# Loading q in two transfers over 128 partitions in place of four over 32

## The chip, the cores and the metric

The kernel runs on one core of a Trainium2 chip. The metric is the device time of one execution in microseconds; less is better. The engines are named as in the profile: PE (matrix multiply; PEld is its weight load), DVE, ACT and POOL (elementwise work), and SP, which computes nothing here and issues the DMA transfers. An engine's name with a q behind it (SPq) means its instruction queue. Transfers are carried by 16 DMA engines that all queues share.

## The reference

Causal attention with a decay for each head and no softmax, for 8 batches of 8 heads, 576 positions and 64 columns; then a feed-forward layer with a squared relu over the 4608 tokens (8 x 576) of 512 columns:

```
scores = scale * np.matmul(q, k.transpose(0, 1, 3, 2))
gamma = 1.0 - 2.0 ** (-5.0 - np.arange(H, dtype=np.float32))
rel = pos[:, None] - pos[None, :]
Dmat = np.where(rel >= 0, gamma[:, None, None] ** rel[None, :, :], 0.0)
ret = scores * Dmat[None, :, :, :]
return np.matmul(ret, v).astype(np.float32)
...
h = x @ w_in
r = np.maximum(h, 0.0)
g = r * r
return (g @ w_out).astype(np.float32)
```

Inputs and output are fp32. w_in is 512 x 2048, w_out 2048 x 512.

## The kernel before

**Units and groups.** The tokens are cut into 36 units of 128 tokens with all 8 heads. A batch has four full units and a tail of 64 positions; the tails of two batches share a unit. So there are 32 full units and 4 tail units. Two units make a group, 18 groups in all. Attention goes chunk by chunk: within a unit the masked scores, and a state R that carries the sum of k times v from chunk to chunk.

**How a unit comes in.** The first 8 units are loaded in pairs (lines 430 to 449) and transposed on PE. The other 28, 24 full and 4 tails, go through `add_load` (lines 411 to 428): SP issues transfers of k, q and v into a slice of the tile `loads`, which has room for five units. Then POOL makes fp16 of it: k by L497 and q by L512 (a multiplication with the decay, two calls of L508 for a tail) into the tile `kq`, v by L518 into `v`. Then SP issues a DMA transpose of `kq` into `kqT` (L529). PE reads `kqT` for the scores (`psc`) and for what comes from the state (`psO`), and `kq` and `v` for the sums of the state (`psS`), all through the helper at L483.

**The layout of q.** For k and v a partition is a token (L422), 8 rows of 256 B for each partition. For q of a full unit the partition 32j + r holds, for the heads j and j + 4, the four tokens 4r to 4r + 3. In HBM four tokens of one head lie together, so each partition is filled by two rows of 1 KB, one of each head. In the slice of `loads` the first half of a partition belongs to the heads 0 to 3 (a = 0), the second to the heads 4 to 7 (a = 1). The layout stays through the transpose and is undone when the result is copied (L889).

**Order.** The order of all work is written out in the list `ORDER`: each entry is a task, each engine executes its tasks in that order, and a task of SP is the whole load of one tensor of one unit. So SP's queue is one fixed sequence of loads, transposes (L529) and stores of the output (L1001, L1006), in which an instruction that waits holds up all behind it. The task of a transpose waits for the POOL tasks of k and q of its unit. The weights come by POOL's queue. SP's transfers take eight semaphores in turn, and each transfer first waits for the one before it on its semaphore, so for the transfer eight places ahead in SP's queue.

**Feed-forward.** The layer is computed group by group, with a recursive seven-product scheme for the second matrix (L1304) and for some of the first (L1058; else L1209), ACT and DVE squaring and adding in between. Its matmuls are placed among the attention of later groups, so PE has work of a group at hand while it is to begin the scores of another, but always in the order of the list.

Of the kernel before, what the change touches and what calls it, by code (L numbers as in the profile page):

```python
# [183 lines left out]
def kernel(  # L184
# [9 lines left out]
    nc = tc.nc  # L194
# [3 lines left out]
    P = 128  # L198
    NP = H // 2
# [199 lines left out]
    def dma_task(key, dur, fn, more=(), **kw):  # L399
        t = add("SP", key, dur, fn, deps=list(last_load) + list(more), **kw)  # L400
        last_load[:] = [t]
        return t
# [8 lines left out]
    def add_load(u):  # L411
        kind, b, c = units[u]
        for n, (name, src) in enumerate((("k", k), ("q", q), ("v", v))):
            def fn(name=name, src=src):
                at = ((u - PAIRED) % LD * 3 + "kqv".index(name)) * H * D
                x = tile_of[name + "32", u] = loads[:, at:at + H * D].rearrange("p (h d) -> p h d", h=H)
                if kind == "full" and name == "q":
                    for j in range(NP):
                        nc.sync.dma_start(out=x[32 * j:32 * j + 32].rearrange("r (a t) d -> r a (t d)", a=2),  # L419
                                          in_=src[b, :, c * P:(c + 1) * P, :].rearrange("(a x) (r t) d -> x r a (t d)", a=2, t=4)[j])  # L420
                elif kind == "full":
                    nc.sync.dma_start(out=x, in_=src[b, :, c * P:(c + 1) * P, :].rearrange("h p d -> p h d"))  # L422
                else:
                    for i in range(2):
                        nc.sync.dma_start(out=x[i * 64:(i + 1) * 64],
                                          in_=src[b + i, :, 512:576, :].rearrange("h p d -> p h d"))
            behind_pair = T["kvx", 6] if PAIRED + 3 <= u < PAIRED + LD else []
            loaded[name, u] = dma_task(0, QL if name == "q" and kind == "full" else 2.2 if (u, name) == (PAIRED, "k") else 1.2, fn, acq=("ld" + name,), more=behind_pair)
# [1023 lines left out]
```

## Time and profile before

| | us |
|---|---|
| three runs | 282.50, 283.57, 286.36 |
| their median | 283.57 |
| the profiled execution, its time | 283.93 |
| its span, first to last instruction | 282.0 |

From the page and its lists, about the steps that the change touches:

| what | value |
|---|---|
| L419, q of 24 full units | 96 transfers of 64 KB; issue 339/427/3097 ns (least, median, most); to landing 1.9/3.4/6.0 us |
| L422, k and v of 24 full units | 24 transfers of 256 KB each; median to landing 4.9 and 4.2 us |
| L425, q of 4 tail units | 8 transfers of 128 KB; median to landing 3.4 us |
| L529, transposes | 28; issue 1232/1517/3114 ns; to landing 3.1/4.4/6.5 us |
| L512 on POOL | 24, median 1045 ns |
| packets on all queues | 119154, 50.03 MB |

How to read it: busy shares are means over the span. A line of the timeline gives start, length, engine, line, operation, and out<-in by the program's names. The chain of waits is followed back from the last instruction; its share of an engine is time in which that engine's work stood between the start and the end. The ends of matmuls are modelled, so PE's busy time may hide short waits. The granted clock of TensorE is 1.00 in every stretch looked at. The DMA share is the recorded time of packets over 16 engines; the records can overlap, so that it may go over 1.

### The profile page before, as it was taken

The page shows a single profiled execution, that of the slowest core. Times are in us where ns is not written, and L with a number is a line of the kernel's source. Part 1 is how long each engine was busy: PE and PEld are TensorE (multiplying, and loading weights), DVE is VectorE, ACT ScalarE, POOL GpSimd, SP SyncE. Part 2 cuts the span into 40 slices and gives each one's busy share as a digit, 9 for nine tenths or more (in the row PEclk, how much of TensorE's full clock was granted, in tenths as well). Part 3 has the DMA queues.
Part 4 walks back from the last instruction along what each step waited for, and adds up shares of the span by engine and source line. Part 5 has one row for each costly group of instructions (what it writes and reads, how often), then busy time and mean ns, then how long its engine had stood idle before and what let it go on. Part 6 is the DMA issues. An engine that isn't in the chain of part 4 may idle for free.

```text
span 282.0 us, 11585 instructions
## 1 busy us (share of the span) xinstructions
PE 273.1 (97%) x4726; PEld 237.5 (84%) x4726; DVE 198.0 (70%) x405; ACT 198.4 (70%) x374; POOL 100.9 (36%) x133
## 2 busy tenths in 40 slices
PE   8989999999999999989999999999999999999994
PEld 3567767888899888979998889898989999999983
DVE  4783379988988568586757595777597777565662
ACT  5657977577578965857797775686888485887831
POOL 7560036353655251455264343365265310000000
PEclk9999999999999999999999999999999999999999
DMA  6999998799999799999979999889979840022114
GB/s 192 300 201 208 246 323 192 171 231 164 195 166 212 166 178 209 222 178 165 230 169 212 195 200 207 210 183 245 182 197 219 155 114 2 5 84 105 40 74 149
DMA packets 119154, 50.03 MB, mean 177 GB/s; under 512 B 94784, under 2 KB 113728, under 8 KB 119104
## 3 DMA queue, kind: packets, MB, share of 16 engines
q1 hardware_dynamic: 114560, 44.84, 74.3%
q0 software_dynamic: 4224, 4.19, 9.1%
q8 instruction: 39, 0.64, 1.0%
q10 hardware_dynamic: 320, 0.26, 0.4%
q14 instruction: 11, 0.09, 0.1%
HBM read 36.70 MB, written 9.44 MB: 164 GB/s over the span
## 4 chain that ended last, share of the span: by engine, by line
PE 63%; DMA 16%; SPq 10%; DVE 4%; POOL 2%; issue 2%; ACT 1%; POOLq 0%; DVEq 0%; ACTq 0%
PE po L1304 28%; PE ph L1209 15%; PE ph L1058 13%; DMA w_out<-in_moe_w_out_dram 5%; SPq L419 5%; DMA loads<-in_q_dram 4%; PE psO L483 3%; DMA pair_c<-in_v_dram 3%; SPq L441 2%; DMA stage<-in_q_dram 2%; DMA kqT<-kq 2%; DMA out_dram<-o 2%; SPq L422 1%; SPq L529 1%; PE psS L483 1%
## 5 line engine op out<-in xcount | busy, mean ns | idle before, releaser
L1209 PE MATMUL ph<-xT,w_in 128*128 128x256 f16 x640 | 83.0, 273 | 0.9 <-DVE xT L713 0.5
L1209 PEld LDWEIGHTS <-w_in 128*128 128x128 f16 x640 | 61.6, 98 | 9.5 <-DMA w_in<-in_moe_w_in_dram 0.5
L1219 ACT ACTIVATE gT<-ph 128x512 f16<-128x512 f32 x80 | 46.2, 597 | 15.6 <-PE ph L1209 15.5
L1304 PEld LDWEIGHTS <-gT 128*128 128x128 f16 x544 | 51.1, 98 | 6.0 <-issue 0.3
L1304 PE MATMUL po<-w_out,gT 128*128 128x256 f16 x272 | 44.8, 273 | 0.0
L1304 PE MATMUL po<-wT,stage 128*128 128x256 f16 x272 | 42.5, 273 | 0.0
L1304 PEld LDWEIGHTS <-stage 128*128 128x128 f16 x408 | 38.1, 98 | 4.6 <-issue 0.2
L1304 PE MATMUL po<-wT,gT 128*128 128x256 f16 x272 | 40.8, 273 | 0.2 <-DVE o L1330 0.2
L1226 ACT ACTIVATE gT<-gT 128x512 f16<-128x512 f16 x66 | 40.0, 631 | 0.4
L497 POOL CAST kq<-loads 128x512 f16<-128x512 f32 x28 | 19.2, 687 | 54.0 <-DMA loads<-in_k_dram 49.6
L1101 ACT ACTIVATE gT<-gT 128x1024 f16<-128x1024 f16 x32 | 33.6, 1059 | 2.7 <-DVE gT L1087 2.6
L512 POOL TENSOR_TENSOR kq<-loads,qexp 128x512 f16<-128x512 f32 x24 | 26.8, 1116 | 22.1 <-DMA loads<-in_q_dram 21.8
L1058 PEld LDWEIGHTS <-pair_c 128*128 128x128 f16 x512 | 32.6, 98 | 1.3 <-issue 0.2
L518 POOL TENSOR_TENSOR v<-loads,vdec_full 128x512 f16<-128x512 f32 x24 | 27.4, 1146 | 10.7 <-DMA loads<-in_v_dram 10.6
L1277 DVE TENSOR_TENSOR stage<-gT,stage 128x512 f16<-128x512 f16 (+1 forms) x51 | 27.9, 561 | 0.8
L1087 DVE CUSTOM_DVE_ANT_0 gT<-ph,parts 128x512 f16<-128x512 f32 x24 | 16.5, 688 | 15.5 <-PE ph L1058 8.1
L1058 PEld LDWEIGHTS <-w_in 128*128 128x128 f16 x384 | 24.7, 98 | 1.2 <-issue 0.4
L1087 DVE CUSTOM_DVE_ANT_0 gT<-ph,stage 128x512 f16<-128x512 f32 x24 | 16.4, 686 | 12.8 <-PE ph L1058 12.3
L1330 DVE TENSOR_TENSOR o<-po,u 128x256 f32<-128x256 f32 x33 | 13.9, 421 | 15.2 <-ACT u L1320 4.7
L889 ACT CAST xT<-psO 128x512 f16<-128x512 f32 x28 | 15.9, 588 | 11.3 <-PE psO L483 11.2
L1320 ACT COPY u<-po 128x256 f32<-128x256 f32 x34 | 12.7, 374 | 12.2 <-PE po L1304 11.4
L1304 PE MATMUL po<-w_out,stage 128*128 128x256 f16 x136 | 21.2, 273 | 0.0
(111 smaller groups left out, 421.8 us busy)
## 6 DMA issues: line engine op xcount, KB each, us to landing
out_dram<-o SPq DMA_DIRECT2D x32, 256.0 KB, 3.1
loads<-in_k_dram SPq DMA_DIRECT2D x24, 256.0 KB, 4.9
loads<-in_q_dram SPq DMA_DIRECT2D x96, 64.0 KB, 3.4
loads<-in_v_dram SPq DMA_DIRECT2D x24, 256.0 KB, 4.2
w_in<-in_moe_w_in_dram POOLq DMA_DIRECT2D x4, 512.0 KB, 8.1
w_out<-in_moe_w_out_dram POOLq DMA_DIRECT2D x4, 512.0 KB, 14.4
pair_c<-in_k_dram SPq DMA_DIRECT2D x2, 512.0 KB, 5.5
pair_c<-in_q_dram SPq DMA_DIRECT2D x4, 256.0 KB, 6.1
```

Of the source, the lines that this page charges most:

```text
L497: op(out=out_.rearrange("p (n b a d) -> p n b a d", n=2, b=2, a=2), in_=in_.rearrange("p (a n b) d -> p n b a d", n=2, a=2))
L512: nc.gpsimd.tensor_tensor(out=out_.rearrange("p (t a d) -> p a t d", t=4, a=2), in0=tile_of["q32", u].rearrange("p (a t) d -> p a t d", a= ...
L518: nc.gpsimd.tensor_tensor(out=t, in0=tile_of["v32", u], in1=vdec[kind].rearrange("p (h o) -> p h o", o=1).to_broadcast([P, H, D]), op=ALU. ...
L889: (nc.scalar.copy if X_ENG[c] == "ACT" else nc.vector.tensor_copy)(out=tile_of["x", g].rearrange("p n (s e r t) -> p e (n s) r t", s=n, e= ...
L1058: nc.tensor.matmul(out_[:, e], lhsT=left[:, m, fi * P:(fi + 1) * P], rhs=right()[:, m], start=fresh and e == 0 and m == 0, stop=m == HK - ...
L1087: nc.vector._custom_dve(TENSOR_ADD_SAT, out=g_at(s, h, j), in0=bank(j, x), in1=part_at[name].rearrange("p (e t) -> p e t", t=P), s0=3.4028 ...
L1101: nc.scalar.activation(out=t, in_=t, func=ACTF.Square)
L1209: nc.tensor.matmul(tile_of["ph", g, fb][:, j, :], lhsT=w_in16[:, m, fi * P:(fi + 1) * P], rhs=tile_of["x", g][:, m, :], start=(m == 0), st ...
L1219: nc.scalar.activation(out=tile_of["g", g][:, nf * fb:nf * (fb + 1), :], in_=tile_of["ph", g, fb], func=ACTF.Relu)
L1226: nc.scalar.activation(out=t, in_=t, func=ACTF.Square)
L1277: (nc.gpsimd if eng == "POOL" else nc.vector).tensor_tensor(out=S_(k)(sl), in0=in0(sl), in1=in1(sl), op=op)
L1304: nc.tensor.matmul(tile_of["pb", g, bank], lhsT=left(i), rhs=right[:, i, :], start=(start and i == 0), stop=(i == HF - 1), skip_group_chec ...
```

## The change

For q of a full unit, the loop over the four head numbers j, each with 32 partitions and both halves, becomes a loop over the two halves a, each with all 128 partitions. The bytes, where they lie in HBM and where they go stay the same, as does everything else.

```diff
                 if kind == "full" and name == "q":
-                    for j in range(NP):
-                        nc.sync.dma_start(out=x[32 * j:32 * j + 32].rearrange("r (a t) d -> r a (t d)", a=2),
-                                          in_=src[b, :, c * P:(c + 1) * P, :].rearrange("(a x) (r t) d -> x r a (t d)", a=2, t=4)[j])
+                    for a in range(2):
+                        nc.sync.dma_start(out=x[:, NP * a:NP * a + NP].rearrange("p t d -> p (t d)"),
+                                          in_=src[b, :, c * P:(c + 1) * P, :].rearrange("(a x) (r t) d -> a x r (t d)", a=2, t=4)[a])
```

In the built programs, with counts from the slowest dimension to the fastest, one transfer of before goes from 32 x 2 x 256 elements in HBM to 32 x 2 x 256 in `loads`; one of the new goes from 4 x 32 x 256 to 128 x 1 x 256. SP issues 204 transfers in place of 252. On the other engines the instructions and their order are the same; what differs is the number of the semaphore that a transfer of SP raises, and that its readers wait for.

## The prediction

> **What bounds the kernel now.** First I read the page's totals, its slices of DMA and its chain.
>
> ```profile
> span 282.0 us, 11585 instructions
> PE 273.1 (97%) x4726; PEld 237.5 (84%) x4726; DVE 198.0 (70%) x405; ACT 198.4 (70%) x374; POOL 100.9 (36%) x133
> ...
> DMA  6999998799999799999979999889979840022114
> ...
> PE 63%; DMA 16%; SPq 10%; DVE 4%; POOL 2%; issue 2%; ACT 1%; POOLq 0%; DVEq 0%; ACTq 0%
> ```
>
> PE is all but full, yet the DMA row stands at 6 to 9 tenths up to slice 32 (to about 225 us), and the chain leaves PE for DMA and SPq over a quarter of the span. So two resources run side by side. The windows tell how close they are (columns: stretch, length, busy us and count of PE, PEld, DVE, ACT, POOL; granted clock; DMA share; GB/s).
>
> ```profile
> 80.00:100.00 20.00, 20.00 (x333) 18.27 (x330) 14.17 (x25) 17.43 (x32) 9.96 (x12) 1.00 1.05 179
> 100.00:120.00 20.00, 19.63 (x438) 18.02 (x436) 14.05 (x29) 13.95 (x25) 7.33 (x10) 1.00 1.13 206
> 120.00:140.00 20.00, 19.07 (x428) 17.24 (x426) 14.00 (x27) 14.16 (x30) 9.60 (x10) 1.00 1.03 193
> ```
>
> PE loses 2.2 us in all between 40 and 240 us (the ten windows of 20 us added up), most of it in the last two rows shown. The cause of that loss is in SP's timeline of one pair of units (start, length, line, form).
>
> ```profile
> 121.79 2.00 SPq L419 DMA_DIRECT2D loads<-in_q_dram  x4
> 123.84 0.43 SPq L422 DMA_DIRECT2D loads<-in_v_dram  x1
> 124.31 0.58 SPq L422 DMA_DIRECT2D loads<-in_k_dram  x1
> 124.93 3.18 SPq L419 DMA_DIRECT2D loads<-in_q_dram  x4
> 128.15 0.43 SPq L422 DMA_DIRECT2D loads<-in_v_dram  x1
> 128.68 0.52 SPq L1001 DMA_DIRECT2D out_dram<-o  x1
> 129.30 1.34 SPq L529 DMA_TRANSPOSE kqT<-kq  x1
> 130.69 0.57 SPq L422 DMA_DIRECT2D loads<-in_k_dram  x1
> 131.37 2.93 SPq L529 DMA_TRANSPOSE kqT<-kq  x1
> ```
>
> The second q load, issued from 124.93 us, landed at 130.07; POOL's L512 ran 130.23 to 131.27; the transpose was issued at 131.37 and landed at 136.76; the scores that read it began at 136.75. So q's load is just in time. The list of waits says the same (who waited for whom: us in total, times, longest).
>
> ```profile
> POOL kq L512 <- DMA loads<-in_q_dram: 21.8, 17, 4.5
> ...
> PE psc L483 <- DMA kqT<-kq: 1.3, 2, 0.9
> ```
>
> Elsewhere a unit's transpose lands earlier: the last one 4.8 us before its scores (227.5 against 232.4). That is the slack at the end.
>
> **What the change takes away.** 96 issues at L419 become 48. In the trace the 96 take 57.7 us of SP together (median 0.43 each, many held up by what is in flight). For the new ones the nearest rows are L441's, 128 partitions with one row each: 0.55 to 0.69 us where not held up. At 0.6, 48 cost 28.8, so SP is relieved of 28.9 us, 1.2 a unit. Every SP transfer also waits for the one eight places ahead of it (eight semaphores); with six transfers a unit instead of eight that wait reaches further back, and I cost it at nothing. None of this shortens PE's own work. At most the 2.2 us that PE loses from 40 to 240 us come back. Lower and upper bound of this part: -2.2 and 0.
>
> **What it adds.** Bytes and packets of data stay: 256 packets of 1 KB a unit, 6144 in all (packet records of the trace). What changes is how a transfer can be shared out. Each of the 252 transfers that SP issues has an outermost count of 32, 64 or 128 on both sides, and ends with sixteen 4-byte finishing packets (4480 on SP's queue: 252 times 16, and 16 more for each of 28 transposes), one to an engine. The new form has 128 partitions on one side, but 4 heads outermost on the other, of which each is 32 rows of 1 KB. No row of before has fewer than 16 outermost. From both sides: it is still split over 16 engines, as L441's is (32 outermost against 128), or over no more than the 4 equal parts that its outermost count gives. I take four, since all the rows shared out to 16 engines have a count that 16 divides, and this one hasn't.
>
> [...]
>
> Now the sum with four engines. Median durations in the packet records: 1 KB 46 ns, 256 B 18 ns, 2 KB 84 ns. A q load is 16 packets an engine now, 0.74 us; on four engines it is 64, 2.94 us, so 2.2 us more a unit, and 24 units put 53.0 us more on each of the four. Room for it: from 40 to 222 us (182 us) all packets at their median durations are 135.4 us an engine; as recorded, 180.0 us. The four then have 135.4 + 53.0 = 188.4 us to do, or, with q's packets at their recorded mean of 63 ns (24.2 us now, 96.8 then), 252.6. In the trace all 192 transfers of this stage whose landing it tells land in the order of their issue, so I take it that k, v, transposes and stores issued behind a q load wait for it on these four, and each is complete only with its last part. The stage of 182 us thus grows by 6.4 us at least and 70.6 at most.
>
> Which value: the recorded sum is too high, since records overlap (shares of 1.05 and 1.13 above, where an engine can't be more than full). The median sum is too low, since the engines also run dry while SP stands at a transpose for POOL: L529 waits 20.1 us for POOL (8.4 + 6.3 + 5.4 by line in the list of waits), with the next loads queued behind. Those waits stay, since each is for a q that lands no sooner. So 188.4 + 20.1 = 208.5, which is 26.5 more than 182. The slack of 4.8 at the end takes some off: 21.7. PE's order is fixed, and the 50 us after the last scores (232 to 282) are untouched, so this goes to the end whole. What hid q's load until now, PE's own 13.2 us a pair of units (scores at 61.1 and 232.4 us, 13 pairs apart), covers it no more: four engines need, at medians, 14.1 us a pair (1.15 each for k, v and transpose, 2.94 for q and 0.67 for the store, twice).
>
> Sum: 282.0 + 21.7 = 303.7 of span. SP's relief is already in the assumption that the engines are otherwise kept fed. The profiled execution took 283.93, 1.9 more than its span, so 305.6; its time is 0.4 above the median of 283.57. I say 306.
>
> **The rivals.**
> 1. Not slower: it is split over 16 engines all the same. For it: L441's sides differ too. Then a load of 128 KB lands as the tails' q loads do (128 KB, 3.4 us in the list of issues), and SP's relief brings 0 to 2.2 us: 281.4 to 283.6. It decides if the finishing packets stay 16 a transfer.
> 2. Four engines, but kept full throughout, the transposes' waits hidden by what is queued: 6.4 - 4.8 = 1.6 us, 285.
> 3. Four engines, at recorded durations: 70.6 - 4.8 = 65.8 more, 349. Against it: with the other twelve engines relieved of q, a packet meets less traffic.
> 4. Faster by more than 2%: SP is what holds PE. For it: SPq has 10% of the chain, L419 4.6% of it. Against it: 2.2 us of idle PE. If half of L419's 13 us of the chain came back, since the ends of matmuls are modelled and may hide waits, it were 277.
>
> **How the numbers follow.** The forecast has 0.80, rival 1 0.11, rival 2 0.04, rival 3 0.02, rival 4 0.03. Anything within 2%, some 5.7 us, of 283.6 can't well be told from no change: that is rivals 1 and 2, 0.15; faster 0.03; slower 0.82. Range: rivals 1, 2 and 4 are left below it (0.18 together), so it begins just above rival 2, at 286. Its upper end lies three quarters of the way from the least growth (6.4) to the most (70.6), since packets meet more traffic than their medians show and less than their means: 54.6 - 4.8 = 49.8 over 283.9, 334.
>
> **What would show it.** Page: 119154 packets become 117810 with four finishing packets a transfer, 118386 with sixteen. The q loads' 128 KB take over 5 us to landing rather than 3.4. PE's waits for kqT grow from 2.8 us (1.5 at the weight loads, 1.3 at the matmuls) to over 20, the scores' pairs are 14 to 16 us apart, and the DMA share falls although the kernel waits for DMA. I am wrong if the packets are 118386, or if PE waits for something other than kqT.

## The result, and the profile after

The changed kernel takes 306.07 us (median of four runs, 301.35 to 307.31) against 284.0 us before. Two of its runs, 307.31 and the profiled one of 306.83, are of a slower state, and every ratio here and below is of the fast runs alone: here 303.3 to 284.2 us, so 1.067, with a 95% interval of 1.050 to 1.085. The forecast was 306, slower by over 2%.

The page of the changed kernel, the parts that answer to those shown of before:

```profile
span 305.1 us, 11514 instructions
PE 281.9 (92%) x4726; PEld 242.7 (80%) x4726; DVE 203.0 (67%) x405; ACT 199.0 (65%) x374; POOL 100.4 (33%) x133
...
DMA packets 117811, 50.03 MB, mean 164 GB/s; under 512 B 93441, under 2 KB 112385, under 8 KB 117761
...
PE 49%; DMA 28%; SPq 12%; POOL 5%; ACT 2%; issue 2%; DVE 2%; POOLq 0%; ACTq 0%
```

The bytes are the same, and the packets are 117811. The prediction gave 117810 for four finishing packets a transfer and 118386 for sixteen, so 47 q transfers or more must have ended with four. The queues' count agrees: 3136 packets of 4 bytes on SP's queue in place of 4480, which is 48 x 4 instead of 96 x 16. The trace's records of packets, each with start and length, tell the same of the data: in the stage of the loads at least one 1 KB packet of a q load is under way for 90.4 us, and the most frequent number at a time is four (for 45.8 us). The chain lies on PE for 49% of the span instead of 63%, and on DMA for 28% instead of 16%.

The windows, with the columns of before:

```profile
80.00:100.00 20.00, 16.22 (x281) 14.59 (x279) 10.50 (x20) 11.54 (x19) 8.35 (x9) 0.83 1.06 156
100.00:120.00 20.00, 20.00 (x430) 18.28 (x428) 14.03 (x29) 14.24 (x30) 6.09 (x9) 1.00 1.00 185
120.00:140.00 20.00, 16.03 (x263) 13.97 (x261) 12.36 (x19) 12.04 (x22) 8.21 (x8) 0.91 0.98 151
```

PE now stands idle for about 4 us in two of these three stretches, and the granted clock falls in the same ones. The rate falls from 179 and 193 GB/s to 156 and 151, while the DMA share stays near 1: that share is a mean over 16 engines and doesn't tell that four have more to do than the rest.

SP's timeline, for the same pair of units as the one shown of before:

```profile
131.49 1.16 SPq L419 DMA_DIRECT2D loads<-in_q_dram  x2
132.70 0.48 SPq L422 DMA_DIRECT2D loads<-in_v_dram  x1
133.22 0.74 SPq L422 DMA_DIRECT2D loads<-in_k_dram  x1
134.01 3.94 SPq L419 DMA_DIRECT2D loads<-in_q_dram  x2
137.99 0.48 SPq L422 DMA_DIRECT2D loads<-in_v_dram  x1
138.57 1.08 SPq L1001 DMA_DIRECT2D out_dram<-o  x1
139.75 2.55 SPq L529 DMA_TRANSPOSE kqT<-kq  x1
```

The first two q transfers take 1.16 us to issue, as costed. The next two take 3.94, though half as many are issued as before; what holds SP there the profile doesn't name. So the relief of SP came to 9.8 us and not 28.9: L419 takes 47.9 us of SP over the run, before it took 57.7.

A stretch of the chain of waits (start, length, what) shows how that reaches PE:

```profile
149.52 3.65 SPq L419
...
153.21 5.52 DMA loads<-in_q_dram
...
158.86 0.51 POOL kq L512
...
159.86 1.04 POOL v L518
160.91 1.03 POOL kq L497
161.93 1.37 SPq L529
...
163.41 3.18 DMA kqT<-kq
...
166.64 0.32 PE psc L483 x16
```

It is 17 us from the issue of one q load to the scores, and 12.4 of them are that issue, its landing and the landing of the transpose. The cast of this q ended at 159.9 us, but its transpose was issued only at 163.41: from 159.58 SP stood in the issue of the transpose of the unit before, so the two other POOL casts in the chain aren't what it waited for.

### The profile page after: what moved, and what is told of

Read it like the earlier page. It is cut to its first block, busy times and chain, and to the rows that moved or that the text cites. A ratio compares the mean times of both kernels' runs of the same rounds, so it can differ in the third digit from the quotient of the medians.

```text
span 305.1 us, 11514 instructions
## 1 busy us (share of the span) xinstructions
PE 281.9 (92%) x4726; PEld 242.7 (80%) x4726; DVE 203.0 (67%) x405; ACT 199.0 (65%) x374; POOL 100.4 (33%) x133
## 2 busy tenths in 40 slices
DMA packets 117811, 50.03 MB, mean 164 GB/s; under 512 B 93441, under 2 KB 112385, under 8 KB 117761
## 4 chain that ended last, share of the span: by engine, by line
PE 49%; DMA 28%; SPq 12%; POOL 5%; ACT 2%; issue 2%; DVE 2%; POOLq 0%; ACTq 0%
PE po L1304 22%; PE ph L1058 11%; PE ph L1209 10%; DMA loads<-in_q_dram 9%; DMA kqT<-kq 5%; DMA loads<-in_k_dram 5%; SPq L419 5%; DMA w_out<-in_moe_w_out_dram 4%; SPq L422 3%; PE warm L392 2%; SPq L529 2%; DMA pair_c<-in_k_dram 2%; PE psO L483 2%; POOL kq L512 2%; DMA loads<-in_v_dram 1%
## 5 line engine op out<-in xcount | busy, mean ns | idle before, releaser
L1209 PEld LDWEIGHTS <-w_in 128*128 128x128 f16 x640 | 62.0, 98 | 9.3 <-issue 0.4
L1304 PEld LDWEIGHTS <-gT 128*128 128x128 f16 x544 | 51.9, 99 | 7.1 <-issue 0.6
L1304 PE MATMUL po<-w_out,gT 128*128 128x256 f16 x272 | 46.3, 280 | 0.0
L1304 PE MATMUL po<-wT,stage 128*128 128x256 f16 x272 | 44.2, 281 | 0.0
L1304 PEld LDWEIGHTS <-stage 128*128 128x128 f16 x408 | 38.8, 100 | 5.6 <-DVE stage L1277 0.3
L1277 DVE TENSOR_TENSOR stage<-gT,stage 128x512 f16<-128x512 f16 (+1 forms) x51 | 31.0, 620 | 0.8
L518 POOL TENSOR_TENSOR v<-loads,vdec_full 128x512 f16<-128x512 f32 x24 | 28.3, 1185 | 4.3 <-DMA loads<-in_v_dram 2.9
L1058 PEld LDWEIGHTS <-w_in 128*128 128x128 f16 x384 | 25.9, 101 | 1.3 <-issue 0.2
L483 PE MATMUL psc<-kqT 64*64 64x64 f16 (+1 forms) x576 | 10.7, 203 | 16.5 <-DMA kqT<-kq 15.3
L1087 DVE CUSTOM_DVE_ANT_0 gT<-ph,stage 128x512 f16<-128x512 f32 x24 | 16.4, 686 | 14.0 <-PE ph L1058 13.6
L483 PEld LDWEIGHTS <-kqT 64*64 64x64 f16 x576 | 7.8, 110 | 18.9 <-DMA kqT<-kq 16.4
```

Of the source, the lines that this page charges most:

```text
L483: t = nc.tensor.matmul(out_, lhsT=lhsT, rhs=rhs, start=start, stop=True, skip_group_check=True, tile_position=(64 * row, 64 * col))
L518: nc.gpsimd.tensor_tensor(out=t, in0=tile_of["v32", u], in1=vdec[kind].rearrange("p (h o) -> p h o", o=1).to_broadcast([P, H, D]), op=ALU. ...
L1058: nc.tensor.matmul(out_[:, e], lhsT=left[:, m, fi * P:(fi + 1) * P], rhs=right()[:, m], start=fresh and e == 0 and m == 0, stop=m == HK - ...
L1087: nc.vector._custom_dve(TENSOR_ADD_SAT, out=g_at(s, h, j), in0=bank(j, x), in1=part_at[name].rearrange("p (e t) -> p e t", t=P), s0=3.4028 ...
L1209: nc.tensor.matmul(tile_of["ph", g, fb][:, j, :], lhsT=w_in16[:, m, fi * P:(fi + 1) * P], rhs=tile_of["x", g][:, m, :], start=(m == 0), st ...
L1277: (nc.gpsimd if eng == "POOL" else nc.vector).tensor_tensor(out=S_(k)(sl), in0=in0(sl), in1=in1(sl), op=op)
```

## The experiments

**How many engines.** Three runs change the outermost count in HBM and nothing else about the bytes and packets of q. The first puts the 32 rows of a head outermost:

```diff
-                                          in_=src[b, :, c * P:(c + 1) * P, :].rearrange("(a x) (r t) d -> a x r (t d)", a=2, t=4)[a])
+                                          in_=src[b, :, c * P:(c + 1) * P, :].rearrange("(a x) (r t) d -> a r x (t d)", a=2, t=4)[a])
```

> Two transfers a q load, over all 128 partitions, as in the changed kernel, but with the 32 rows of a head outermost in HBM in place of the 4 heads (32 x 4 x 256 to 128 x 256). The tokens of q so land in other partitions than the readers take them from, so the output is that of another order of q; bytes, packets, instructions and their order are those of the changed kernel. Theory A (a transfer is shared out over as many engines as its outermost counts allow, and four engines are what costs the time): 16 engines again, 281 to 284 us, 118386 packets on the page, 16 finishing packets a transfer. Theory B (it is the form that costs: two transfers of 128 KB with unlike sides land later and are issued more slowly, however they are shared out): 300 to 306 us, as changed.

Measured 283.55 us, 0.999 of before (0.995 to 1.002). The DMA part of its page:

```profile
DMA packets 118386, 50.03 MB, mean 177 GB/s; under 512 B 94016, under 2 KB 112960, under 8 KB 118336
```

That is the count for sixteen finishing packets. It is two transfers of 128 KB over 128 partitions, in the same places of SP's queue as the changed kernel's, and the loss is gone. Theory B falls.

The second has eight outermost:

```diff
-                                          in_=src[b, :, c * P:(c + 1) * P, :].rearrange("(a x) (r t) d -> a x r (t d)", a=2, t=4)[a])
+                                          in_=src[b, :, c * P:(c + 1) * P, :].rearrange("h (a r t) d -> a h r (t d)", a=2, t=4)[a])
```

> Two transfers a q load over 128 partitions, each of 8 heads x 16 rows x 256 elements, so eight outermost. The tokens of q again land elsewhere, so the output is that of another order. Theory A: eight engines, 32 packets an engine and load, 1.47 us; the eight have 135.4 - 17.7 + 35.3 = 153.0 us to do, with SP's 20.1 of waits 173, under the 182 of the stage: 282 to 286 us, 118002 packets. Theory B: 300 to 306 us.

Measured 282.82 us, 0.996 of before (0.993 to 0.999), with the 118002 packets of eight:

```profile
DMA packets 118002, 50.03 MB, mean 178 GB/s; under 512 B 93632, under 2 KB 112576, under 8 KB 117952
```

So eight finishing packets a transfer, by my reading eight engines, carry it at no loss. The third goes back to four transfers of 64 KB, with two heads outermost in each:

```diff
                     for a in range(2):
-                        nc.sync.dma_start(out=x[:, NP * a:NP * a + NP].rearrange("p t d -> p (t d)"),
-                                          in_=src[b, :, c * P:(c + 1) * P, :].rearrange("(a x) (r t) d -> a x r (t d)", a=2, t=4)[a])
+                        for i in range(2):
+                            nc.sync.dma_start(out=x[64 * i:64 * i + 64, NP * a:NP * a + NP].rearrange("p t d -> p (t d)"),
+                                              in_=src[b, :, c * P:(c + 1) * P, :].rearrange("(a i x) (r t) d -> a i x r (t d)", a=2, i=2, t=4)[a, i])
```

> Four transfers a q load as before the change, of 64 KB each, but each over 64 partitions from 2 heads x 32 rows x 256 elements, so two outermost; q lands where it should. Theory A: two engines, 128 packets an engine and load, 5.9 us; the two have 135.4 - 17.7 + 141.3 = 259 us to do in place of 135.4, at least 72 us more than the 182 of the stage after the slack of 4.8, and 92 with SP's waits: 354 to 376 us, 117810 packets. Theory B: four transfers of 64 KB like before, 283 to 290 us.

Measured 358.25 us, 1.262 of before (1.255 to 1.268). Four transfers of 64 KB are as many and as large as before the change, so neither number nor size is the cause. The page has 117810 packets, which is two finishing packets for each of the 96 transfers, and while q's 1 KB packets are under way (147.3 us), two stand at a time for 111.9 us. PE's waits for the transposes, from its list of waits (its lines lie one further down):

```profile
PEld L484 <- DMA kqT<-kq: 45.6, 13, 8.5
PE psc L484 <- DMA kqT<-kq: 44.1, 13, 8.4
```

16, 8, 4 and 2 engines thus give 283.6, 282.8, 306.1 and 358.3 us: flat where the few engines' packets, at their medians, fit into the stage (153.0 of 182 us for eight), and steep where they don't (188.4 for four, 259 for two). Two engines have 259 us to do at the medians; from the first q issue at 39.9 us to the last transpose at 299.3 it took 259.4.

**A version that keeps two transfers and sixteen engines.** The rows are outermost as in the first run, and the readers follow: `qT` takes every fourth column, and the decay of q is built for that order.

```diff
+        if units[u][0] != "tail" and u >= PAIRED:
+            return t.rearrange("p n (r x) -> p n r x", x=NP)[:, :, 16 * c:16 * c + 16, x]
```

> Two transfers a q load over 128 partitions with the 32 rows outermost, and all readers adapted: the decay of q is built for that order at the start, and the scores and the state's part read q's columns with a step of four. Theory A: 280 to 284 us, at best 2.2 us under before, if the reads with a step cost PE nothing. Theory B: 300 to 306 us.

Measured 285.91 us, 1.007 of before (1.004 to 1.010): no gain. The scores on PE (the least, median and most ns of one, in that kernel's lines) tell why it isn't even equal:

```profile
L490 PE MATMUL psc<-kqT x576: 186/234/311, 10.1 to 236.1; 64*64 64x64 f16 x149, 64*64 64x128 f16 x43
```

Before the change the median of the same 576 was 193 ns. The reads with a step of four columns took longer here, PE's busy time is 278.3 us against 274.2 in the first run, and PE is what is full.

**Is it the engines' time, or only q's own landing?** k and v of the full units are read as 128 rows of 2 KB, on the changed kernel and on the one before:

```diff
-                    nc.sync.dma_start(out=x, in_=src[b, :, c * P:(c + 1) * P, :].rearrange("h p d -> p h d"))
+                    nc.sync.dma_start(out=x.rearrange("p h d -> p (h d)"), in_=src[b].rearrange("h (p e) d -> (h p) (e d)", e=8)[c * P:(c + 1) * P])
```

> The changed kernel, with k and v of the 24 full units read as 128 rows of 2 KB that lie together in HBM, in place of 1024 rows of 256 B: the same bytes, issues and order, but other tokens and heads reach the partitions, so the output isn't that of the reference's k and v. At the medians of the packet records that is 8 packets of 84 ns an engine and load, 0.67 us, in place of 1.15, so 23.0 us less on every engine over the 24 units. q's transfers stay as changed. Theory A1 (the four engines' time in all is the limit): 188.4 - 23.0 + 20.1 = 185.5 us of the 182, less than the slack: 283 to 288 us. Theory A2 (the engines have time to spare, and only q's own later landing counts, since SP and POOL wait for it in turn): 300 to 306 us, as changed.

> The kernel before the change with the same edit of k and v as in the run beside it, whose control it is; again other tokens and heads reach the partitions. Both theories: no limit of DMA is to be lifted beyond the 2.2 us that PE loses, so 281 to 284 us.

Measured 286.64 us (1.003 of before, 0.998 to 1.008) with the change, and 283.31 us (0.994, 0.990 to 0.998) without. q's transfers are those of the changed kernel, which by the packet count used four engines, with 64 packets on each for a load, and the loss falls from 6.7% to 0.3% (1.0% against its control) when k and v take 23 us less of these engines, at the packets' medians. So A1: it is the sum of what stands on the four. PE waits little for the transposes then:

```profile
PEld L483 <- DMA kqT<-kq: 3.4, 5, 1.4
...
PE psc L483 <- DMA kqT<-kq: 2.6, 3, 1.3
```

**What fills the time above the medians' sum.** The prediction put 20.1 us of SP's waits at the transposes on top of the 188.4. Six runs were meant to see whether that is so. In the first two, ACT's queue issues q, once with four engines and once with sixteen:

```diff
-                        nc.sync.dma_start(out=x[:, NP * a:NP * a + NP].rearrange("p t d -> p (t d)"),
+                        nc.scalar.dma_start(out=x[:, NP * a:NP * a + NP].rearrange("p t d -> p (t d)"),
```

> The changed kernel with the 48 q transfers issued by ACT's queue in place of SP's, so that they no longer stand behind a transpose that waits for POOL, nor k and v behind them in one queue; the work is the same. Theory C (the 20.1 us of the prediction's sum are engines run dry while SP stands at a transpose): much of them comes back, 286 to 296 us, if ACT can spare the issues (the control beside it tells). Theory D (the four engines are kept full, and what exceeds 188.4 us is packets that take longer than their median in the traffic): 300 to 306 us.

> The control for the run beside it: two transfers with the 32 rows outermost, so sixteen engines, issued by ACT's queue; the tokens of q land in other partitions, so the output is that of another order of q. Both theories: what ACT's 48 issues cost by themselves, 0.6 us each, 28.8 us of an engine that is busy 198 of 282: 282 to 290 us.

Measured 317.28 us (1.112, 1.103 to 1.120) and 291.76 us (1.031, 1.027 to 1.035). ACT's issues cost 8 us by themselves, more than expected, and neither theory had the first time. By the ratios the two are 8.1% of before apart, the changed kernel and the first run above 6.8%. But it isn't the same loss, as the waits of the first of the two show:

```profile
PE ph L1209 <- ACT xT L889: 6.9, 2, 5.1
...
PEld L483 <- DMA kqT<-kq: 2.0, 2, 1.3
...
PE psc L483 <- DMA kqT<-kq: 1.8, 2, 1.2
```

PE hardly waits for transposes there. It waits for ACT, 24 us in all, and ACT, which now issues q, itself waits 27.0 us for q's transfers (in the control not at all). So this pair decides nothing about theory C.

A cleaner one shortens what SP waits for: POOL's multiplications become casts.

```diff
-                nc.gpsimd.tensor_tensor(out=out_.rearrange("p (t a d) -> p a t d", t=4, a=2),
-                                        in0=tile_of["q32", u].rearrange("p (a t) d -> p a t d", a=2),
-                                        in1=by.rearrange("p (a t o) -> p a t o", a=2, o=1).to_broadcast([P, 2, 4, D]), op=ALU.mult)
+                nc.gpsimd.tensor_copy(out=out_.rearrange("p (t a d) -> p a t d", t=4, a=2),
+                                      in_=tile_of["q32", u].rearrange("p (a t) d -> p a t d", a=2))
...
-            nc.gpsimd.tensor_tensor(
-                out=t, in0=tile_of["v32", u],
-                in1=vdec[kind].rearrange("p (h o) -> p h o", o=1).to_broadcast([P, H, D]), op=ALU.mult)
+            nc.gpsimd.tensor_copy(out=t, in_=tile_of["v32", u])
```

> The changed kernel with POOL's two multiplications a full unit (L512 for q, L518 for v, 1.05 us each) replaced by plain casts of the same shapes (0.61 us by L497's row): the decay factors of q and v are left out. Each unit's transpose so waits up to 0.87 us less for POOL, 21 us over 24 units. Theory C (SP's waits for POOL at the transposes are what the four engines lose above 188.4 us): 288 to 298 us. Theory D (they are not): 302 to 306 us.

> The kernel before the change with the same plain casts on POOL, as the control for the run beside it; the decay factors of q and v of full units are left out here too. Both theories: 281 to 284 us, since PE's own work sets the end.

Measured 304.59 us (1.071, 1.065 to 1.077) and 284.51 us (1.001, 0.997 to 1.005). SP's waits at the transposes, as the lists of SP's own waits give them, first of the changed kernel, then of this one (the transpose is L526 here):

```profile
SPq L529 <- POOL v L518: 14.0, 8, 3.2
SPq L529 <- POOL kq L497: 10.4, 6, 3.9
SPq L529 <- POOL kq L512: 3.0, 3, 1.3
```

```profile
SPq L526 <- POOL kq L497: 8.1, 5, 3.4
SPq L526 <- POOL v L517: 6.8, 5, 2.8
SPq L526 <- POOL kq L512: 2.8, 4, 1.0
```

By these lists 27.4 us became 17.7, and the ratio stayed within its interval (1.071 against 1.067). But the lists give more than SP waited: the largest entry is v's cast, and a transpose waits for the casts of k and q alone. The same holds of the 8.4 + 6.3 + 5.4 us in the prediction, for instance at the transpose issued at 131.37 us before the change (start, length):

```profile
130.23 1.04 POOL L512 TENSOR_TENSOR kq<-loads,qexp 128x512 f16<-128x512 f32 x1
131.36 2.56 POOL L518 TENSOR_TENSOR v<-loads,vdec_full 128x512 f16<-128x512 f32 x2
```

The cast of its q was done at 131.27, and SP, free since 131.26, issued it 0.1 us later; the list puts 2.6 us down to v's casts, which ended during the issue. All 28 transposes of before start after their own casts, and in SP's timeline the gaps ahead of them that end with a cast are 2.5 us in all. They are 6.3 us with the change and 2.0 here. So theory C falls: there were no 20 us of such waits to lose.

Last, each transpose is issued as two:

```diff
-            nc.sync.dma_start_transpose(out=t, in_=tile_of["kq", u].rearrange("p x n -> p (x n)"))
+            for i in range(2):
+                nc.sync.dma_start_transpose(out=t[:, NP * i:NP * i + NP], in_=tile_of["kq", u][:, i])
```

> The changed kernel with each of the 28 transposes at L529 issued as two, one for k's half and one for q's, with the same packets; the result is the same. In the packet records of before, 435 packets of 256 B, some 16 a transpose, take over 200 ns each, 408 us together, so 25.5 us an engine; with the change 511 and 752 us. Theory H (each transpose holds every engine for about 0.9 us at its start, and that is what the four engines lose above 188.4 us): 28 starts more, so 20 to 25 us more, 322 to 332 us, and about 900 such packets. Theory D' (the hold is that of engines that wait for others, and costs the four nothing): 303 to 310 us.

> The kernel before the change with each transpose issued as two, as the control for the run beside it. Theory H: 135.4 us at the medians and twice 25.5 of holds are 186.4 on every engine, over the 182 of the stage but within the slack: 284 to 292 us. Theory D': 282 to 286 us.

Measured 316.82 us (1.113, 1.104 to 1.121) and 308.64 us (1.082, 1.074 to 1.089). Both lie outside what either theory gave. The long packets became fewer, not more: 326 over 200 ns with the change, 156 without. So they are no fixed hold at the start of a transpose, and theory H falls; theory D' fails in its times. The records do show what the long packets wait with: in the changed kernel those of one transpose begin up to 3.4 us apart and end within 60 ns of one another. One q load's packets stood from 54.9 to 58.6 us; seventeen long packets began between 55.7 and 56.9, four more at 58.3 to 58.5, and all ended at 59.0. That looks like the other engines waiting at a transpose for the four that still have q, though the records don't tell the engine.

What goes with the time of the second kernel is the issue of its transposes (SP, least, median and most ns):

```profile
L530 SPq DMA_TRANSPOSE kqT<-kq x56: 1188/1218/2202, 49.3 to 254.4; - x56
```

Half a transpose takes as long to issue as a whole one at its least (1232 ns before), so SP issues transposes for 72.7 us instead of 48.1, and the last of them is issued 30 us later (254.4 against 224.4). The 24.6 us more of issuing and the 24.2 us more of time agree, and no packet at all is under way for 11.7 us of the stage, 0.5 before. That SP's queue is what costs the time is argued from this; no run lengthened its issuing alone.

## Why the prediction was right

- *PE nearly full, q's load just in time.* Held, though not at once: the first two pairs of units on this path began their scores at 61.0 and 73.7 us (61.1 and 73.2 before), and PE's first wait for a transpose of the new loads ended at 90.7, after 3.7 us.
- *Four engines, by the outermost count of 4.* When it was taken no row had fewer than 16 outermost, so it was an estimate. The runs bear it out at the counts they had: with 32, 8, 4 and 2 outermost in HBM a q transfer ended with 16, 8, 4 and 2 finishing packets (118386, 118002, 117811 and 117810 packets on the pages); with 4 and 2, four and two packets of data were most often under way at a time (45.8 of 90.4 us, 111.9 of 147.3); and the times, 283.6, 282.8, 306.1 and 358.3 us, follow the work of the few. That a finishing packet stands for an engine is read from these together, as the records don't name the engine, and no run shows what other counts do.
- *SP's relief, 28.9 us of issuing, brings 0 to 2.2 us.* The gain held, the 28.9 didn't. With sixteen engines the relief is 15.9 us (L419 takes 41.8), and the time stays within its interval of before. With four it is 9.8.
- *The floor of 6.4 us and the ceiling of 70.6.* The stage grew by 25.2 us: the last transpose was issued at 249.6 us in place of 224.4. Predicted were 26.5. The eight-engine run agrees with the same sum: 153 of 182 us, and no loss. The two-engine run agrees with it to 0.4 us without any addition.
- *20.1 us for SP's waits at the transposes.* This step failed in its cause. Its size was right: the four had 188.4 us to do at the medians, and it took 209.3 from the first q issue (40.3) to the last transpose (249.6), 20.9 more. But the 20.1 us weren't waits: SP stood 2.5 us ahead of transposes for a cast of q, 6.3 with the change. With two engines the list has 20.4 us of the same entries (13.6 + 4.2 + 2.6), and the medians' sum comes out without them. That the forecast came out at 306, and not at rival 2's 285, rests on a term whose cause was another: that is luck.
- *The slack of 4.8 taken off once, the rest to the end whole.* The last scores began at 255.5 us in place of 232.4, 23.1 later (predicted 21.7), and from there to the end it is 49.6 us in both. The span is 305.1 against 303.7.
- *What would show it.* PE's waits for kqT are 16.4 at the weight loads and 15.3 at the matmuls, mostly the same time seen twice, where the prediction added both. The pairs are 15.0 us apart in the mean over 13 (61.0 to 255.5), but from 10.2 to 21.6 singly (9.5 to 17.1 before), and not 14 to 16. q's transfers land 5.6 us after their issue in the median, by the last raise of their semaphore, so over 5 as said. The DMA share fell little: 1.01 in the mean of the three windows, 1.07 before.

Open is why the stage took 20.9 us more than the medians' sum. The packet records tell where it stands. From 40.3 to 249.6 us a packet of a q load is under way for 90.4 us, where 24 times 2.94 is 70.6; the rest takes 118.9 us, where the medians give 117.8. With the plain casts it is 95.6 of 207.8 us, and with two engines 147.3 of 259.4, where the medians give 141.3; the rest is 112 in both. So the excess lies with q's loads themselves. Their packets take 54 ns in the mean and not the median's 46, and for 27 of the 90 us fewer than four are under way, so the four don't start and end together; why, isn't shown. It isn't that all engines run dry: some packet is under way in all but 0.7 of the 209 us. Nor is it shown to be SP: its issues take 169 of the 185 us from 40 to 225 before the change and 170 with it, though half as many are for q, so much of that is waiting (at each line's least time they would take 110 and 88 us).

## What to carry to other kernels

When transfers are merged, look at the outermost count of both sides: here 8, 4 and 2 outermost in HBM, against 128 partitions (64 with two), left a q transfer with as many finishing packets and so, by my reading, on as many DMA engines, and with four the last transpose was issued 25.2 us later. Work out then what the busiest engine has to do in the stage, and not the mean over 16; here there was no loss where that was below the stage's time (153 of 182 us: 0.996 of before), and above it nearly all arrived (of the 25.2 us with four, 23.1 at the last scores). The page's packet count tells, once the packets of data are taken off and the rest is divided by the number of transfers, how many finishing packets a transfer had (16, 8, 4 and 2 here), before any time is read. And a list of waits can put a wait down to work that nobody needed (20.1 us listed before the change, 2.5 us stood): look in the timeline whether the engine stood idle at all.

## What the runs showed of the hardware

The granted clock of PE was 1.00 between 20 and 275 us before. With the change it falls to half in four stretches of that time, one of 6.8 us and three of 3.4, each beginning while PE waits for a transpose or up to 1.5 us after such waits (of up to 3.7 us); with two engines it is half for 61.4 us before the last scores, in stretches of 3.4, 6.8 and 10.2. The waits ahead can be short: before the stretch at 167.6 us PE waited 1.7 and 0.9 us, with matmuls between. After the wait of 1.6 us at 210.2 the clock stayed at 1.00, and what decides between the two isn't shown. PE's busy time grew by 8.8 us for the same 4726 matmuls. None of it shows after the last scores, and what it cost before them wasn't measured.

An issue of a transpose by SP took 1.19 us at the least for 128 x 512 elements and 1.23 for 128 x 1024, and 48 issues of plain transfers moved to ACT's queue cost the kernel 8 us.
